# An RWKV-6 layer with a gated MLP on one core: level six and the state's products of steps six to eleven in one TensorE group

## The chip, the cores and the metric

The kernel runs on one core of one Trainium2 chip. The metric is the time on the device in microseconds, the median over runs. All arithmetic is fp32.

## The reference

Two blocks follow one another. The first is the RWKV-6 recurrence for 4 batches, 8 heads, 768 tokens and head size 48:

```
state = 0
for t in range(768):
    cur   = (u * k[t]) outer v[t]
    y[t]  = r[t] @ (state + cur)
    state = w[t][:, None] * state + k[t] outer v[t]
```

The decay w lies between 0.80 and 0.95 and differs by token and by channel. The second block takes the 3072 x 384 result x through a hidden layer of 2048:

```
h   = x @ w_in
g   = h * erf(softplus(h))
out = g @ w_out
```

## The kernel before, in words

The 768 tokens are cut into six chunks of 128, the four batches into two pairs, which makes twelve steps, numbered 0 to 11. A step takes one chunk of two batches: 256 token rows, 16 batch-head pairs. Steps with the same parity belong to the same pair of batches, so the state made in step s is used in step s + 2.

Inside a chunk the recurrence is a triangular matrix of products between receptances r and keys k, each faded by the decays between the two tokens. The kernel builds it in levels: level n pairs the left half of a block of 2^n tokens with its right half. A chunk is split into two halves of 64 tokens, so level six is the last. `level_products` makes a level's products on TensorE, `take_level` puts them into the tile `own` (a masked copy on VectorE up to level five, two plain copies on ScalarE for level six), and `scale` multiplies r and k of the next step's tile `in` by the products of decays that the level asks for. GpSimd makes those products of decays (`tot_sb`).

From step 5 on (`attend_late`), the levels one to four are not made by TensorE. Instead `prepare(s + 1)`, a generator, works in step s on the near products of the next step: for each distance 1 to 15 inside a block of 16 tokens it multiplies r by shifted keys (`term`, lines 463 and 467), sums over channels (`sum_up`, line 453), and fades the keys one token further. VectorE does the distances 1 to 4, GpSimd 5 to 15. The sums (`sums`) and the faded keys (`words`) then go through DRAM to be turned around: `k_blocks` and `by_blocks` are written, `by_tokens` and `kT` are read back, all on SyncE's queue (lines 499 to 509). `by_tokens` gives the first content of the next step's `own` (line 514). `kT` holds keys faded to the end of their block of 16; they still have to be faded to the end of their half of 64. For that `spread_blocks` turns `over_blocks`, a small tile of decay products, with a matmul against the identity, ScalarE copies the result (`few`), and two transfers spread it to every token (`g_rows`, `spread`). Line 718 multiplies `kT` by `spread`.

The products of faded keys with values give what a half adds to the state (`state_part`, line 659). The sums are `middle`, the state in the middle of the chunk (line 736), and `S_next`, that at its end (line 743), each from an old state faded by GpSimd (`faded`, lines 713 and 739) and the products in PSUM. `from_own` (line 584) and `through_state` (line 610) of a step run at the head of the following step: they make y in PSUM, the first from `own` and the values, the second from the states and r. `fence` (line 593) is a small VectorE copy between the two halves of `from_own`.

The MLP runs two and three steps behind, cut into pieces that are placed by hand between the groups of the attention. A letter string for each stage of a step says which pieces stand there:

- P: one of seven pieces of a projection (`project_fast`, line 1142), 16 matmul records of 192 columns
- H: one of eight pieces of the hidden layer (`hidden`, line 1027), 12 matmul records of 256 columns, with a ScalarE copy that empties the PSUM tile (line 1036); two such tiles (`m`) take turns
- s, ey, ep: softplus of a chunk, and erf of it into the PSUM lane y or the PSUM lane p, each with an activation table load on ScalarE
- m: VectorE's multiply of a chunk by its erf (line 992)
- k22y, k11p, k12y: ScalarE copies of quarters of a hidden tile into a lane (line 1100); S1 to S4: VectorE's sums of quarters (lines 1119 to 1125) for the projection
- F: one more part of `prepare`
- w: one sum of weights for the last two steps' hidden layer (line 1194)

The lane p is the PSUM tile pp1, the level products use pp0, and the lane y is the tile in which y is made. Each engine runs its instructions in the order in which they are written here; the stages of a step are "front", "near" and 0 to 4. The usual strings before the change are

```python
USUAL = (
    "s P", "m", "ey P m s P P ep P", "m k22y P F P k11p F F", "S1", "S2 S3 H k12y S4 H F",
    "s H ey m H H F s H ep H H",
)
```

Of the kernel before, what the change touches and what calls it, by code (L numbers as in the profile page):

```python
# [11 lines left out]
FP32 = mybir.dt.float32  # L12
# [49 lines left out]
def kernel(  # L62
# [47 lines left out]
    faded = [const.tile([P, JP, D], FP32, name="faded")] * NC  # L110
    seen = const.tile([P, NE * NP * NC], FP32, name="seen")

    over_blocks = const.tile([P, C // NEAR, JP], FP32, name="over_blocks")
    u_sb = const.tile([P, NP], FP32, name="u_sb")
    ident = const.tile([P, P], FP32, name="ident")
    mask_sb = const.tile([P, MASKED, HC], I32, name="mask_sb")
# [14 lines left out]
    def products(shape, n=None):  # L131


        if n is not None:
            return ps_p.tile(shape, FP32, name=f"pp{n}")
        n = turns["next"]
        turns["next"] = 1 - n
        return ps_p.tile(shape, FP32, name=f"pp{n}")
# [65 lines left out]
    def near_log(s):  # L204
        return NEAR_LOG - (s == DIRECT)
# [97 lines left out]
    def rows(e, n=D):  # L303
        return slice(e * EP, e * EP + n)
# [7 lines left out]
    def scale(s, level, batch=None):  # L312

        in_t, tots = loaded[s][0], ready[s][1]
        half, nb = 1 << (level - 1), JP * C >> level
        if batch is not None:
            nb //= NJ
            halves = view(
                turns["first"][:, batch], half, [[NP * C - half, 2], [2 * half, nb], [1, half]]
            )  # L320
            nc.vector.tensor_mul(
                halves, halves,
                view(tots[level - 1], 2 * batch * nb, [[1, 2], [2, nb], [0, half]]),
            )
            return
        n = 1 if s > DIRECT and level == LOG else 2
        halves = view(in_t[:, 0:2], half, [[JP * C - half, n], [2 * half, nb], [1, half]])
        nc.vector.tensor_mul(  # L328
            halves, halves, view(tots[level - 1], 0, [[1, n], [2, nb], [0, half]])
        )  # L330
# [23 lines left out]
    def prepare(s):  # L354
# [61 lines left out]
        if s == DIRECT:  # L416
            yield
        else:
            half = view(tots[NEAR_LOG + 1], 1, [[2, NC], [C >> NEAR_LOG + 1, JP]])
            quarter, last = (  # L420
                view(tots[NEAR_LOG], n, [[4, NC], [C >> NEAR_LOG, JP]]) for n in (1, 3)
            )
            to = over_blocks[:].rearrange("p (h b) n -> p b h n", h=NC)
            nc.gpsimd.tensor_mul(to[:, 0], quarter, half)
            nc.gpsimd.tensor_copy(out=to[:, 1], in_=half)
            nc.gpsimd.tensor_copy(out=to[:, 2], in_=last)
            yield
# [79 lines left out]
        if near == NEAR:  # L507
# [2 lines left out]
                out=kTs[s][:], in_=k_blocks[:].rearrange("(g b) s d -> (b s) g d", g=NH)  # L510
            )
        scale(s, near_log(s))
        nb = HC // NEAR
        nc.vector.tensor_mul(
            own[:].rearrange("p n (b t) -> p n b t", t=NEAR),
# [148 lines left out]
                        stop=True,  # L664
                    )

    def spread_blocks(s, pp):


        n = D // 2  # L670
        for e in range(NE):
            nc.tensor.matmul(
                pp[:EP, e, 0:2, HC // 2 : HC // 2 + n],
                lhsT=over_blocks[rows(e)].rearrange("p b n -> p (b n)"),
                rhs=ident[rows(e), rows(e)], start=True, stop=True,
            )
        few = att.tile([EP, NE * 2, n], FP32, name="few", bufs=1)
        nc.scalar.copy(
            few[:].rearrange("p (e i) d -> p e i d", e=NE),
            pp[:EP, :, 0:2, HC // 2 : HC // 2 + n],  # L680
        )
        g_rows = dram.tile([C // NEAR, JP * NE * D], FP32, name="g_rows")
        nc.sync.dma_start(
            out=g_rows[:].rearrange("b (n d) -> (b n) d", n=JP),
            in_=few[:].rearrange("p i d -> p (i d)"),
        )
        spread[s] = att.tile([P, JP, NE, D], FP32, name="spread", bufs=1)
        nc.sync.dma_start(
            out=spread[s][:].rearrange("p n e d -> p (n e d)"),
            in_=g_rows[:, None, :].to_broadcast([C // NEAR, NEAR, JP * NE * D]),  # L690
        )

    def attend_late(s, run):

        c, in_t, vt, own, S, S_next, ends = parts_of(s)
        RK = by_pair(in_t)
        before = s - 1 if s - 1 > DIRECT else None
        if before:
            from_own(before, ready[before][0], 1)
            fence()  # L700
        pp = products([P, NE, JP, HC], 0)
        level_products(pp, RK, LOG - 1)
        scale(s, LOG - 1)
        take_level(own, pp, LOG - 1)
        run("front", None)
        if before:
            from_own(before, ready[before][0], 0)
            through_state(before, xTs[before])
            if s + 1 < n_steps:
                load_step(s + 1)  # L710
        following = prepare(s + 1) if s + 1 < n_steps else iter(())
        next(following, None)
        nc.gpsimd.tensor_mul(faded[0][:], S[:], ends[:, :, 0:1].to_broadcast([P, JP, D]))
        next(following, None)
        run("near", None)
        next(following, None)
        kT = kTs[s]
        nc.vector.tensor_mul(
            kT[:].rearrange("p (e n) d -> p n e d", e=NE),
            kT[:].rearrange("p (e n) d -> p n e d", e=NE), spread[s][:],  # L720
        )
        run(0, following)

        pp = products([P, NE, JP, HC], 0)
        level_products(pp, RK, LOG)
        if s + 1 < n_steps:
            spread_blocks(s + 1, pp)
        take_level(own, pp, LOG)
        scale(s, LOG)
        run(1, following)  # L730
        ps = products([P, NC, JP, HC], 0)
        ps = [[ps[:, h]] * NE for h in range(NC)]
        state_part(s, kT, ps)
        run(2, following)
        for e in range(NE):
            nc.vector.tensor_add(middle[rows(e)], faded[0][rows(e)], ps[0][e][rows(e), :, :D])
        run(3, following)
        if s < n_steps - SPC:
            nc.gpsimd.tensor_mul(
                faded[1][:], middle[:], ends[:, :, 1:2].to_broadcast([P, JP, D])  # L740
            )
            for e in range(NE):
                nc.vector.tensor_add(S_next[rows(e)], faded[1][rows(e)], ps[1][e][rows(e), :, :D])
        run(4, following)

    def attend_first(xT):

# [572 lines left out]
    def in_order(s, k):  # L1320
# [3 lines left out]
        for what in order[k]:  # L1324
# [5 lines left out]
                piece(hids, s - 1)  # L1330


    STAGES_LATE = ("front", "near", 0, 1, 2, 3, 4)
    LATE = {
        DIRECT + 1: (
            "s ey", "m", "s ep m P P s ey m P P P", "s P F ep m P F P k22y k11p F", "S1",
            "S2 S3 H k12y S4 H F", "s H ep m H H F G s H H H ep",
        ),
        n_steps - 1: (
            "s P", "m w", "ey P m s P P ep P", "m P P", "", "", ""  # L1340
        ),
    }
    USUAL = (
        "s P", "m", "ey P m s P P ep P", "m k22y P F P k11p F F", "S1", "S2 S3 H k12y S4 H F",
        "s H ey m H H F s H ep H H",
    )

    def run_late(s, tokens, following=None):
# [64 lines left out]
    with tc.manual_schedule(  # L1413
# [74 lines left out]
        s = n_steps  # L1488
        from_own(s - 1, ready[s - 1][0], 1)
        fence()  # L1490
        run_late(s - 1, "S Q w w w")
        from_own(s - 1, ready[s - 1][0], 0)
        through_state(s - 1, xTs[s - 1])
        run_late(s, "P P P P T")
# [102 lines left out]
```

## Time and profile before

| what | value |
|---|---|
| time, median of 3 runs | 584.82 us (583.95 to 585.79) |
| profiled execution, its own time | 586.88 us |
| its span from the first to the last instruction | 585.1 us |
| TensorE busy | 576.4 us, 99% |
| VectorE busy | 454.7 us, 78% |
| ScalarE busy | 355.6 us, 61% |
| GpSimd busy | 274.1 us, 47% |
| starts of steps 6 to 11 (first `from_own` record) | 240.98, 285.73, 330.23, 374.73, 419.23, 463.71 us |

In the order of time of an engine a row gives the start in us from the beginning of the span, the duration of that run of instructions, the engine and the line, what is written and what is read, and in brackets how long the engine had been idle and what ended that. Merged rows can overlap the following row by a little, so lengths of pieces are taken from one start to the next. An fp32 matmul leaves two records. Busy time is an average over the whole execution: in the stretch of steps 6 to 11 VectorE is busy for some 40 of every 44.5 us.

### The profile page before, as it was taken

How to read it: one execution, taken by the hardware profiler on the slowest of the kernel's cores; microseconds unless marked ns; L12 is line 12 of the kernel's file. 1: busy time of each engine (PE TensorE's matmuls, PEld its weight loads, DVE VectorE, ACT ScalarE, POOL GpSimd, SP SyncE). 2: the span in 40 equal slices, each digit the busy share in tenths (PEclk: the TensorE clock that was granted, in tenths of full speed). 3: DMA queues.
4: the chain of work that ended last, by engine and by line, in shares of the span. 5: the costliest groups of instructions: out<-in, count | busy, mean ns of one | idle time of the engine just before them, and what ended most of it. 6: DMA issues, size and time to landing. Idle time of an engine off the chain costs nothing.

```text
span 585.1 us, 16663 instructions
## 1 busy us (share of the span) xinstructions
PE 576.4 (99%) x7240; PEld 495.1 (85%) x7240; DVE 454.7 (78%) x558; ACT 355.6 (61%) x478; POOL 274.1 (47%) x313
## 2 busy tenths in 40 slices
PE   8899999999999999999999999999999999999997
PEld 6588887688668758998898898898898899988997
DVE  6776886999996899799799799799799637256630
ACT  3658877644544598756766666665765771387700
POOL 4557391702398469659459459449549200000000
PEclk9999999999999999999999999999999999999999
DMA  8587571440433414334334334334331301000000
GB/s 269 177 273 281 201 235 44 183 154 10 145 95 116 117 55 156 63 116 165 74 111 169 74 108 172 75 108 136 74 108 55 74 8 36 2 0 2 28 27 29
DMA packets 54082, 63.25 MB, mean 108 GB/s; under 512 B 35160, under 2 KB 40568, under 8 KB 52984
## 3 DMA queue, kind: packets, MB, share of 16 engines
q1 hardware_dynamic: 53624, 61.98, 33.4%
q8 instruction: 57, 0.93, 0.6%
q10 hardware_dynamic: 384, 0.20, 0.1%
q14 instruction: 17, 0.14, 0.1%
HBM read 52.39 MB, written 8.69 MB: 104 GB/s over the span
## 4 chain that ended last, share of the span: by engine, by line
PE 95%; DVE 3%; issue 1%; ACT 0%; POOL 0%; DVEq 0%; POOLq 0%
PE m L1027 36%; PE m L1142 28%; PE m L1059 8%; PE pp L552 6%; PE pp L1230 4%; PE y L1230 2%; PE y L584 2%; PE pp L659 2%; PE y L610 2%; PE m L862 1%; PE pp L871 1%; PE pp L938 1%; DVE in L328 1%; DVE words L467 1%; PE pp L1142 0%
## 5 line engine op out<-in xcount | busy, mean ns | idle before, releaser
L1027 PE MATMUL m<-xT,w_in_sb 128*128 128x256 f32 x960 | 215.3, 382 | 0.1
L1027 PEld LDWEIGHTS m<-xT,w_in_sb 128*128 128x128 f32 x960 | 179.9, 190 | 26.2 <-issue 1.0
L328 DVE TENSOR_TENSOR in<-in,tot_sb 128x1024 f32<-128x1024 f32 (+1 forms) x55 | 75.3, 1369 | 16.5 <-PE pp L552 13.2
L463 POOL TENSOR_TENSOR rk<-words 128x528 f32<-128x528 f32 (+3 forms) x28 | 42.5, 1517 | 91.2 <-DVE sums L453 80.7
L1036 ACT COPY h<-m 128x512 f32<-128x512 f32 x80 | 46.4, 579 | 57.6 <-PE m L1027 57.5
L467 POOL TENSOR_TENSOR words<-words,rest 128x528 f32<-128x528 f32 (+10 forms) x77 | 78.1, 1015 | 6.0
L1059 PE MATMUL m<-w_out_sb,h 128*128 128x384 f32 x192 | 64.3, 491 | 0.0
L1059 PEld LDWEIGHTS m<-w_out_sb,h 128*128 128x128 f32 x192 | 35.7, 190 | 23.5
L1142 PE MATMUL m<-mixed,h 128*128 128x192 f32 x256 | 45.6, 331 | 0.0
L1142 PE MATMUL m<-w_out_sb,h 128*128 128x192 f32 x256 | 44.8, 329 | 0.0
L552 PEld LDWEIGHTS pp<-in 48*64 48x64 f32 (+1 forms) x2368 | 33.4, 126 | 12.0 <-issue 6.2
L1142 PEld LDWEIGHTS m<-mixed,h 128*128 128x128 f32 x256 | 41.4, 190 | 0.9
L1142 PEld LDWEIGHTS m<-w_out_sb,h 128*128 128x128 f32 x256 | 41.6, 190 | 0.3
L1142 PE MATMUL m<-w_out_sb,room 128*128 128x192 f32 x240 | 41.5, 326 | 0.0
L983 ACT ACT_TABLE_LOAD x30 | 38.5, 1283 | 2.7 <-issue 2.2
L987 ACT ACT_TABLE_LOAD x30 | 38.5, 1283 | 1.5 <-DVE room L1125 1.1
L1142 PEld LDWEIGHTS m<-w_out_sb,room 128*128 128x128 f32 x240 | 39.4, 190 | 0.0
L402 POOL TENSOR_TENSOR tot_sb<-tot_sb 128x256 f32<-128x256 f32 (+4 forms) x50 | 36.2, 724 | 3.8
L552 PE MATMUL pp<-in 48*64 48x32 f32 (+1 forms) x2368 | 37.3, 212 | 0.6 <-DVE in L328 0.5
L463 POOL TENSOR_TENSOR words<-words 128x336 f32<-128x336 f32 (+6 forms) x49 | 35.3, 720 | 3.8
L453 DVE TENSOR_REDUCE sums<-rk 128x14 f32<-128x672 f32 (+9 forms) x54 | 34.7, 701 | 0.0
L453 DVE TENSOR_REDUCE sums<-words 128x6 f32<-128x288 f32 (+8 forms) x66 | 26.9, 464 | 3.9 <-POOL words L463 3.6
(198 smaller groups left out, 951.5 us busy)
## 6 DMA issues: line engine op xcount, KB each, us to landing
in<-in_rkw SPq DMA_DIRECT2D x8, 1024.0 KB, 5.1
words<-in_moe_w_in SPq DMA_DIRECT2D x16, 384.0 KB, 5.4
words<-in_moe_w_out SPq DMA_DIRECT2D x16, 384.0 KB, 4.7
words<-in_rk_rows SPq DMA_DIRECT2D x8, 768.0 KB, 5.6
w<-in_rkw SPq DMA_DIRECT2D x11, 512.0 KB
v<-in_v SPq DMA_DIRECT2D x12, 384.0 KB, 5.6
out<-o SPq DMA_DIRECT2D x23, 192.0 KB, 2.4
in<-in_rkw SPq DMA_DIRECT2D x7, 512.0 KB, 5.7
```

What stands on the lines that cost most here:

```text
L328: nc.vector.tensor_mul(halves, halves, view(tots[level - 1], 0, [[1, n], [2, nb], [0, half]]))
L402: nc.gpsimd.tensor_mul(new, pair[:, :, 0], pair[:, :, 1])
L453: nc.vector.tensor_reduce(out=view(sums[:], n, [[near * (NEAR + 1), NEAR // near], [NEAR + 1, near - n]]), in_=terms[n], axis=mybir.AxisLi ...
L463: engine.tensor_mul(terms[n], r[:, :, n:], k[:, :, : near - n])
L467: engine.tensor_mul(k[:, :, :m], k[:, :, :m], w[:, :, n : n + m])
L552: nc.tensor.matmul(to, lhsT=rk(1, n)[rows(e), s0 : s0 + m], rhs=right, start=True, stop=True,)
L983: nc.scalar.activation(sp_room, chunks[0], AF.Softplus)
L987: nc.scalar.activation(at, sp_room, AF.Erf)
L1027: nc.tensor.matmul(ps[:, ff, :], lhsT=w_in_sb[:, g * FG + f + ff, kk * P : (kk + 1) * P], rhs=xT[:, kk, :], start=kk == 0, stop=kk == KT - 1,)
L1036: nc.scalar.copy(h[:, f : f + FT, :], ps[:])
L1059: nc.tensor.matmul(ps[j][:], lhsT=gs[g][:, f, j * C : (j + 1) * C], rhs=w_out_sb[:, g * FG + f, :], start=g + f == 0, stop=g == NG - 1 and ...
L1142: nc.tensor.matmul(to, lhsT=a[:, f], rhs=b[:, f], start=start and f == 0, stop=f == FG - 1, skip_group_check=True,)
```

## The change

From step 6 on, five things are different.

1. The level-six products and the state's products follow one another directly, in a new stage "mid" behind `through_state`, with the piece "ey P" in front of them. The state's products are written to pp1, since pp0 holds level six. ScalarE's two copies of level six stand between the first erf (ey) and the softplus of stage 0.
2. `spread_blocks` stays at its place, now alone among projection pieces, as one matmul of 128 rows and 96 columns against the identity in place of two of 48 rows. For this `over_blocks` has 128 columns.
3. The state's sums (`sum_states`) stand together before the near sums of the next step. The fading of `middle` for `S_next` goes from GpSimd to VectorE, in step 5 too.
4. The multiply of `kT` by `spread` (`fade_keys`) is written at the end of the step before, behind the multiply of the last erf (lane p) and the first content of `own`, for which `prepare` has one more `yield`.
5. In step 11 the one w of the stage "near" goes to the tail, where four stand together.

Step 5 keeps its order, but for the sums and for its last stage, where the second ep stands one H piece earlier and m and F follow.

```diff
@@ prepare @@
         scale(s, near_log(s))
+        yield
         nb = HC // NEAR
@@ spread_blocks @@
+        if pp is None:
+            got = products([P, NE * JP * HC], 0)[:, : NE * D].rearrange("p (e d) -> p e d", e=NE)
             nc.tensor.matmul(
-                pp[:EP, e, 0:2, HC // 2 : HC // 2 + n],
-                lhsT=over_blocks[rows(e)].rearrange("p b n -> p (b n)"),
-                rhs=ident[rows(e), rows(e)], start=True, stop=True,
+                got, lhsT=over_blocks[:].rearrange("p i b n -> p (i b n)"),
+                rhs=ident[:].rearrange("p (e m) -> p e m", e=NE)[:, :, :D],
+                start=True, stop=True,
             )
+            nc.scalar.copy(few[:], got[:EP])
...
@@ attend_late @@
+        run("mid", None)
+
+        def state():
+            ps = products([P, NC, JP, HC], 1 if before else 0)
+            state_part(s, kTs[s], [[ps[:, h]] * NE for h in range(NC)])
+            return ps
+
+        def sum_states(ps):
+            for h, into in enumerate((middle, S_next)):
+                if h and s >= n_steps - SPC:
+                    continue
+                if h:
+                    nc.vector.tensor_mul(
+                        faded[1][:], middle[:], ends[:, :, 1:2].to_broadcast([P, JP, D])
+                    )
+                for e in range(NE):
+                    nc.vector.tensor_add(
+                        into[rows(e)], faded[h][rows(e)], ps[rows(e), h, :, :D]
+                    )
+
+        if before:
+            pp = products([P, NE, JP, HC], 0)
+            level_products(pp, RK, LOG)
+            ps = state()
+            take_level(own, pp, LOG)
         following = prepare(s + 1) if s + 1 < n_steps else iter(())
         next(following, None)
         nc.gpsimd.tensor_mul(faded[0][:], S[:], ends[:, :, 0:1].to_broadcast([P, JP, D]))
         next(following, None)
         run("near", None)
+        if before:
+            sum_states(ps)
         next(following, None)
-        kT = kTs[s]
-        nc.vector.tensor_mul(
-            kT[:].rearrange("p (e n) d -> p n e d", e=NE),
-            kT[:].rearrange("p (e n) d -> p n e d", e=NE), spread[s][:],
-        )
+        if not before:
+            fade_keys(s)
         run(0, following)
...
+        elif s + 1 < n_steps:
+            spread_blocks(s + 1)
         scale(s, LOG)
...
         run(4, following)
+        for _ in following:
+            pass
+        if s + 1 < n_steps:
+            fade_keys(s + 1)
+
+    def fade_keys(s):
+
+        kT = kTs[s][:].rearrange("p (e n) d -> p n e d", e=NE)
+        nc.vector.tensor_mul(kT, kT, spread[s][:])
@@ the strings @@
-    STAGES_LATE = ("front", "near", 0, 1, 2, 3, 4)
+    STAGES_LATE = ("front", "mid", "near", 0, 1, 2, 3, 4)
     USUAL = (
-        "s P", "m", "ey P m s P P ep P", "m k22y P F P k11p F F", "S1", "S2 S3 H k12y S4 H F",
-        "s H ey m H H F s H ep H H",
+        "s P", "ey P", "", "m s P P ep P", "m k22y P F P k11p F F", "S1", "S2 S3 H k12y S4 H F",
+        "s H ey m H H F s H ep H H m F",
     )
-        run_late(s - 1, "S Q w w w")
+        run_late(s - 1, "S Q w w w w")
```

## The prediction

> **What bounds the kernel now.** I read the page first, then the order of time of each engine over one whole step (step 8, which begins at 330.23 us), then the transfers. The page's chain of waits:
>
> ```profile
> PE 95%; DVE 3%; issue 1%; ACT 0%; POOL 0%; DVEq 0%; POOLq 0%
> ```
>
> TensorE sets the end. Its order of time over step 8 (start, duration, instruction):
>
> ```profile
> 331.73 2.87 PE L1142 MATMUL m<-w_out_sb,h 128*128 128x192 f32 x16
> ...
> 346.61 0.76 PE L552 MATMUL pp<-in 48*32 48x32 f32 x64
> 347.30 0.32 PE L672 MATMUL pp<-ident,over_blocks 48*64 48x48 f32 x4
> 347.55 2.87 PE L1142 MATMUL m<-mixed,h 128*128 128x192 f32 x16
> ...
> 352.94 0.94 PE L659 MATMUL pp<-v,kT 64*48 64x48 f32 x64
> 353.81 20.99 PE L1027 MATMUL m<-xT,w_in_sb 128*128 128x256 f32 x96
> 374.73 0.66 PE L584 MATMUL y<-own,v 64*48 64x64 f32 x32
> ```
>
> There is no hole: a step lasts 374.73 - 330.23 = 44.50 us. So cheaper TensorE work pays in full, but only while VectorE keeps up. VectorE and GpSimd over the same step:
>
> ```profile
> 333.62 0.94 DVE L470 TENSOR_TENSOR words<-words,u_row 128x768 f32<-128x768 f32 x1
> ...
> 341.29 1.21 DVE L992 TENSOR_TENSOR h<-h,pp 128x1024 f32<-128x1024 f32 x1
> 342.42 2.37 DVE L453 TENSOR_REDUCE sums<-rk 128x15 f32<-128x720 f32 x3
> ...
> 347.22 1.72 DVE L718 TENSOR_TENSOR kT<-kT,spread 128x768 f32<-128x768 f32 x1
> ...
> 357.71 1.21 DVE L1119 TENSOR_TENSOR room<-h,y 128x1024 f32<-128x1024 f32 x1
> 358.84 1.11 DVE L736 TENSOR_TENSOR middle<-faded,pp 48x384 f32<-48x384 f32 x2
> ```
> ```profile
> 343.40 1.31 POOL L463 TENSOR_TENSOR rk<-words 128x528 f32<-128x528 f32 x1 [14.52 <-DVE sums L453]
> ...
> 366.69 0.28 POOL L467 TENSOR_TENSOR words<-words,rest 128x48 f32<-128x48 f32 x1
> ```
>
> GpSimd's near products of step 9 start 0.98 us after VectorE's first sums (342.42) and keep it going to 366.97. Then SyncE's queue takes the finished keys through DRAM:
>
> ```profile
> 367.00 0.33 SPq L499 DMA_DIRECT2D k_blocks<-words  x1
> 367.45 0.36 SPq L501 DMA_DIRECT2D by_blocks<-sums  x1
> 369.74 0.37 SPq L503 DMA_DIRECT2D by_tokens<-by_blocks  x1
> 370.21 0.99 SPq L509 DMA_DIRECT2D kT<-k_blocks  x1
> ```
> ```profile
> kT<-k_blocks SPq DMA_DIRECT2D x1, 384.0 KB, 4.7
> ```
>
> The keys land at 370.21 + 4.7 = 374.9, just after step 9 began, yet line 718 first needs them a whole stage later, some 17 us of slack. In step 6 (from 240.98) ScalarE shows a second place where little is left:
>
> ```profile
> 270.28 1.02 ACT L1100 COPY y<-h 128x1024 f32<-128x1024 f32 x1 [2.24 <-DVE room L1119]
> 271.23 0.58 ACT L1036 COPY h<-m 128x512 f32<-128x512 f32 x1
> ```
>
> The copy that empties a hidden layer's PSUM tile stands behind a lane copy, and that waits for S1 (line 1119) on VectorE. The second hidden piece's tile was ready at about 269.9 and is read until 271.81; the fourth piece, 2.6 us behind the third, needs it at 272.5.
>
> **What the Trainium skill says.** "TensorEngine Tiling (Array Packing)", Key Properties: a change of tiling mode drains TensorE. The trace agrees in direction: a projection piece between two of its own kind takes 2.60 us from start to start (338.72, 341.32), one between two small groups 2.79 (331.73 to 334.52). "SBUF — State Buffer", Who interferes with whom: a VectorE instruction with two SBUF inputs and a GpSimd instruction that reads SBUF exclude each other for a whole instruction. The trace agrees: line 718 takes 1.72 us beside GpSimd and 0.96 in step 11, where GpSimd rests. "DMA: Bandwidth & Descriptors", Anatomy of one DMA: about 2 us of a transfer are fixed. The 16 KB xT transfers take 1.9 us to land, so a shorter wait for kT can't be hoped for.
>
> **The change part by part.** Sums go against the profiled execution (span 585.1, its time 586.88, 2.06 above the median 584.82); the difference goes onto the median.
>
> *TensorE.* Matmuls keep their number but for the spread, four records of 48 rows (0.25 us, 347.30 to 347.55) that become two of 128 rows and 96 columns. The trace has no such form. The nearest row is the projection's, 16 records of 192 columns in 2.60 us, 0.1625 each: two cost 0.16 us if time goes with the columns and 0.33 if the weight load sets it; I take 0.20, nearer the columns, because small groups show that loads can run faster than 0.16 each. Level six and the products are adjacent: 0.69 + 0.87 kept. Of the seven projection pieces (18.78 us in step 8) two now stand between small groups (2 x 2.79), one behind one (2.71), four between their own kind (4 x 2.60): 18.69. The hidden pieces lose the switch at their front: 20.92 to 20.82. Step: 44.50 - 0.05 - 0.09 - 0.10 = 44.26. Bounds: 0 to 0.4 saved.
>
> *ScalarE.* The same copies, softplus and erf. Level six's two copies (1.16 us) now wait for TensorE, done 9.3 us into the step; softplus with its table load (2.3) then ends at 13.0, and the piece's copy behind it (0.46) by 13.5. The piece that needs that copy starts at 15.4: hidden by two pieces, dear only if ScalarE is 1.9 us late.
>
> *VectorE.* The fading of S_next moves here from GpSimd (0.83 there): line 467 takes 0.76 for 576 columns and 0.90 for 720, so 384 come to some 0.57 (between 0.50, in proportion, and GpSimd's 0.83). The state's sums are 1.14 + 0.59 + 1.13 = 2.86 and now stand ahead of the near sums, where a 1.13 multiply stood: those, and GpSimd behind them, start 1.7 later. The multiply of the second erf, own (now no longer waiting for by_tokens in the middle of the step) and line 718 go to the end of the step before. Line 718 waits there for kT, and behind it in VectorE's queue stand the fence, scale of level five, level five's masked copy and everything of the next step. That closes a loop which had been open.
>
> *The loop*, from the end f of line 718 to the next: fence 0.20 + scale 1.14 + copy 0.61 = 1.95; nine near products 341.29 - 333.62 = 7.67; state sums 2.86; to GpSimd's start 0.98; GpSimd 23.60 (343.40 to 367.00) less some 0.58, because line 718 no longer takes the port from it (the 480-column product beside it took 1.80 against 1.22): 23.02; k_blocks to kT's issue 3.21; landing 4.7 + 0.19 (own starts at 372.93, by_tokens landed 3.0 after 369.74); line 718 beside an idle GpSimd 0.90. Sum 45.48 us, 1.22 above TensorE's 44.26.
>
> *Where TensorE meets it.* S1 starts at f + 12.48 (to the near sums) + 4.80 (rest of sums, 342.42 to 347.22) + 1.13 + 0.60 + 1.13 + 0.46 + 1.64 + 0.46 + 3.42 (the rows from 348.86 to 357.71) = f + 26.12. Then 1.24 to the lane copy, 0.95 + 0.58 for it and the hidden copy behind it, 0.1: the fourth hidden piece starts at f + 29.0. Softplus (2.25 with its table load) and a copy (0.6) stand before the fifth, so 31.85 where TensorE was ready at 31.6; erf and a copy before the sixth, 34.7 for 34.45. With five pieces of 2.61 and those 0.5 the step ends at f + 42.6. The fence needs f + 0.3 at 4.3 us into the step, level six f + 2.0 at 8.6: with f 2.9 us into the step both are in time.
>
> *Course.* In step 5 the sums inserted delay the near sums to 235.9, so by_blocks goes then, by_tokens 2.2 later, kT 0.47, and f(6) = 238.5 + 4.7 + 0.19 + 0.90 = 244.3. Step 7 begins at 244.3 + 42.6 = 286.9 (285.73 before), step 8 at 332.4 (330.23), step 9 at 377.9, step 10 at 423.3 (419.23). In step 10 half the state falls away, 1.72 us less, so step 11 begins one free TensorE step later, 467.6 (463.71 before): +3.9. Step 11 has no near products and no loop; it and the tail cost 0.05 less. The join of weights moved to the tail adds 1.2 us on VectorE ahead of the tokens' joins; those end at 498.96 and TensorE wants the first at 504.86: hidden by 5.9. Median 584.82 + 3.85 = 588.7 us.
>
> **The rivals.**
> *A, the loop decides* (my case): a loop L from 44.7 to 46.2 gives, by the same course, a step 11 1.5 to 6.0 later and 586.3 to 590.8. For it: every row of the loop is in the trace. Against: 1.22 is the small difference of two large sums.
> *B, the loop closes inside TensorE's step* (not slower). Place: line 718's wait for kT. It needs a loop of at most 44.3, that is 1.2 us less: near products or GpSimd faster where they no longer share the port. Then 0.24 for six steps, and 0.25 of a ScalarE wait in step 6: some 583.2; half closed, 585.
> *C, the loop is longer.* GpSimd keeps 23.6, and its totals of the next step run beside line 718 (1.64): L = 46.8. Step 11 then begins at 244.3 + 4 x 46.8 + 40.9 = 472.4: +8.7, 593.5.
> *D, the copy of level six holds up ScalarE*: softplus waits for TensorE's group, pieces wait for their copy. Above a lateness of 1.9 us each counts; 0.7 us in six steps less the gain gives 588. Nothing in the rows asks for it.
> That the group doesn't come together isn't a case: both products are issued in one run.
>
> **How the numbers follow.** A 0.68, B 0.17, C 0.11, D 0.04. What a measurement can tell from no change is 0.3%, 1.75 us: 583.1 to 586.6. B lies around the lower edge: 0.06 faster, 0.11 same; A's low end gives 0.04 to same. Faster 0.06, same 0.15, slower 0.79. A's own range is 586.3 to 590.8; with most of B and up to C, 583.6 to 593.5.
>
> **What would show it.** Right: VectorE idle ahead of line 718 "DMA kT", about 1 us a step; TensorE's step 45.3 to 45.6 in steps 7 to 9 with holes in the hidden pieces (line 1027's idle put down to ScalarE's h), and 44.3 in step 11; GpSimd's first product some 14.7 us into a step instead of 13.2; the hidden row of 96 at 20.8 where nothing waits. Wrong: TensorE whole at 44.3 with kT landed ahead of line 718 (B), holes at the fence or level five (C), holes in the projection pieces (D).

## The result, and the profile after

The changed kernel takes 588.81 us (587.45 to 589.34, median of 6 runs) against 585.41 us (583.95 to 586.12, 6 runs) for the kernel before: a ratio of 1.0058, interval 1.0041 to 1.0075. It is slower, by some 3.4 us. A repetition beside the experiments gave 587.82 against 585.05, ratio 1.0041 (1.0029 to 1.0053). The profiled execution took 588.25 us, with a span of 586.4.

Up to the first projection record of step 5 the change hardly touches the kernel, and yet the profiled executions of this case differ there by 3 us (it stands at 194.1 to 197.2 us). So the parts of two profiles are compared from that record on. "Repeated" is a second profiled execution of the changed kernel.

| us | before | changed | changed, repeated |
|---|---|---|---|
| rest of step 5 | 43.82 | 45.56 | 44.75 |
| steps 6 to 10 | 222.73 | 225.02 | 224.93 |
| step 11 | 23.16 | 23.32 | 23.32 |
| the tail | 98.23 | 98.20 | 98.20 |
| sum | 387.94 | 392.10 | 391.20 |

The repeated execution is 3.26 us longer: 0.93 in step 5, 2.20 in steps 6 to 10, 0.16 in step 11, less 0.03 in the tail. The first one has a further 0.8 in step 5. Of the other kernels with the same step 5 one has it too (45.53), the rest take 44.70 to 44.97; in the two long ones S1 stands 28.23 and 28.26 us behind the first projection record, in the repeated execution 27.27. The lengths of steps 6 to 10 are

| us | 6 | 7 | 8 | 9 | 10 |
|---|---|---|---|---|---|
| before | 44.75 | 44.50 | 44.50 | 44.50 | 44.48 |
| changed | 45.45 | 45.02 | 45.05 | 45.07 | 44.43 |
| changed, repeated | 45.48 | 45.04 | 45.07 | 45.08 | 44.26 |

In the rows of a profile PE is TensorE and PEld its weight loads, DVE is VectorE, ACT ScalarE, POOL GpSimd, and SP SyncE; a q behind the name stands for the engine's queue. L1061 is line 1061 of that kernel's text; the lines of the kernels differ by some numbers. The page's chain of waits of the changed kernel, shares of the span by engine:

```profile
PE 53%; DVE 7%; ACT 3%; issue 2%; DMA 1%; ACTq 0%; SPq 0%; DVEq 0%
```

TensorE had 95% of this chain, and now VectorE, ScalarE and a transfer stand in it. (Followed back from the end it reaches only to about 195 us here, so its shares add up to some 66%.) TensorE's order of time over step 8 (start, duration, instruction):

```profile
330.35 0.66 PE L585 MATMUL y<-own,v 64*48 64x64 f32 x32
...
338.93 0.76 PE L553 MATMUL pp<-in 48*32 48x32 f32 x64
339.62 0.94 PE L660 MATMUL pp<-v,kT 64*48 64x48 f32 x64
340.49 2.87 PE L1176 MATMUL m<-w_out_sb,room 128*128 128x192 f32 x16
...
348.39 0.36 PE L674 MATMUL pp<-ident,over_blocks 128*128 128x96 f32 x2
348.58 2.79 PE L1176 MATMUL m<-mixed,h 128*128 128x192 f32 x16
351.21 2.76 PE L1176 MATMUL m<-w_out_sb,h 128*128 128x192 f32 x16
353.81 21.66 PE L1061 MATMUL m<-xT,w_in_sb 128*128 128x256 f32 x96
375.40 0.67 PE L585 MATMUL y<-own,v 64*48 64x64 f32 x32
```

The group is there: level six and the state's products take 0.69 and 0.87, start to start, and the spread 0.19 as two records. Up to the hidden layer nothing is late: it begins 23.46 us into the step (23.58 before). But its 96 records last 21.59 us from start to start where before they lasted 20.92. The waits of steps 7 to 9 say for whom (engine, line, cause: us in total, times, longest):

```profile
PEld m L1061 <- ACT h L1070: 3.5, 9, 0.4
...
DVE kT L778 <- DMA kT<-k_blocks: 1.2, 3, 0.5
```

Three times a step a hidden piece, the fourth, the fifth and the sixth, waits for the copy that empties its PSUM tile. And once a step VectorE waits for kT. VectorE's order of time over the same step (in brackets: idle before, and what ended it):

```profile
330.93 0.96 DVE L778 TENSOR_TENSOR kT<-kT,spread 128x768 f32<-128x768 f32 x1 [0.34 <-DMA kT<-k_blocks]
331.80 0.17 DVE L594 COPY seen<-y 128x16 f32<-128x16 f32 x1
331.99 1.23 DVE L328 TENSOR_TENSOR in<-in,tot_sb 128x1024 f32<-128x1024 f32 x1
...
341.42 1.11 DVE L734 TENSOR_TENSOR middle<-faded,pp 48x384 f32<-48x384 f32 x2
...
344.31 2.38 DVE L453 TENSOR_REDUCE sums<-rk 128x15 f32<-128x720 f32 x3
...
350.37 1.50 DVE L328 TENSOR_TENSOR in<-in,tot_sb 128x512 f32<-128x512 f32 x1
...
358.90 1.21 DVE L1153 TENSOR_TENSOR room<-h,y 128x1024 f32<-128x1024 f32 x1
...
373.28 1.22 DVE L1026 TENSOR_TENSOR h<-h,pp 128x1024 f32<-128x1024 f32 x1 [2.96 <-ACT pp L1021]
374.42 1.22 DVE L515 TENSOR_TENSOR own<-block_sb,by_tokens 128x1024 f32<-128x1024 f32 x1
376.12 0.96 DVE L778 TENSOR_TENSOR kT<-kT,spread 128x768 f32<-128x768 f32 x1 [0.48 <-DMA kT<-k_blocks]
```

Line 778 is the multiply that was line 718, line 1153 is S1, and lines 730 and 734 are the state's sums. Two closed ways lead from this step into the next.

*The kT loop.* From line 778 (330.93) to scale (331.99), the near products, the state's sums, the near sums (344.31), GpSimd's start (345.29), its end and k_blocks (368.22), kT's issue (371.43) and 4.69 us later line 778 again: 376.12 - 330.93 = 45.19, and 44.94 in the step before. The mean, 45.07, is the step. The rows of GpSimd's start and of SyncE's queue:

```profile
345.29 1.31 POOL L463 TENSOR_TENSOR rk<-words 128x528 f32<-128x528 f32 x1 [16.80 <-DVE sums L453]
```
```profile
368.22 0.33 SPq L499 DMA_DIRECT2D k_blocks<-words  x1
...
371.43 1.05 SPq L509 DMA_DIRECT2D kT<-k_blocks  x1
```

*The S1 loop.* From the step's start (330.35) 1.64 to scale, which needs TensorE's level five; 26.91 to S1; 1.24 to ScalarE's lane copy (360.14); 0.96 to the copy of the second hidden piece behind it (361.10), which takes 0.58; and from its end the fourth hidden piece and what follows, some 13.7 to the next start at 375.40. Sum 45.05. ScalarE works without a gap from the lane copy to the copy ahead of the sixth hidden piece (366.80), so a later S1 also comes through to the sixth piece, the last that waits. The first two rows of ScalarE:

```profile
360.14 1.02 ACT L1134 COPY y<-h 128x1024 f32<-128x1024 f32 x1 [2.96 <-DVE room L1153]
361.10 0.58 ACT L1070 COPY h<-m 128x512 f32<-128x512 f32 x1
```

In the kernel before the second way was 1.64 + 25.84 + 1.24 + 0.95 + 0.58 + 13.7 = 43.95: half a microsecond of slack under TensorE's 44.50. The stretch from scale to S1 grew by 1.07: 2.89 for the state's sums, less 1.64 (line 718 gone) and 1.13 (a multiply gone), and 0.8 for a row whose work nobody changed, level six's scale (128 x 512), which took 0.60 from start to start before and takes 1.41 now; 0.14 are small differences of other rows, most of it in the near sums.

Both loops share the stretch from scale to the near sums on VectorE, and both have the length of the step. Which of them holds it can't be read from this profile: that is what most experiments are for.

Step 5 has a hole of its own. ScalarE and TensorE there:

```profile
229.02 1.28 ACT L1021 ACT_TABLE_LOAD   x1 [0.83 <-DVE h L1157]
```
```profile
231.91 8.04 PE L1061 MATMUL m<-xT,w_in_sb 128*128 128x256 f32 x36 [0.81 <-ACT h L1070]
```

The first erf of the lane p waits for S3 (line 1157), which reads that lane, and a hidden piece's copy stands behind the erf. S3 now starts 5.15 us behind S1 (227.73 - 222.58) and started 3.41 behind it before (227.90 - 224.49), since all the state's sums stand between S1 and S2, where only those of `middle` stood.

### The profile page after: what moved, and what is told of

The parts are those of the page before. It is cut to its first block, busy times and chain, and to the rows that moved or that the text cites. A ratio compares the mean times of both kernels' runs of the same rounds, so it can differ in the third digit from the quotient of the medians.

```text
span 586.4 us, 16630 instructions
## 1 busy us (share of the span) xinstructions
PE 578.0 (99%) x7230; PEld 493.6 (84%) x7230; DVE 457.5 (78%) x563; ACT 356.9 (61%) x478; POOL 264.8 (45%) x308
## 4 chain that ended last, share of the span: by engine, by line
PE 53%; DVE 7%; ACT 3%; issue 2%; DMA 1%; ACTq 0%; SPq 0%; DVEq 0%
PE m L1176 25%; PE m L1061 17%; PE pp L1264 4%; PE y L1264 2%; DVE in L328 2%; PE pp L553 1%; DVE sums L453 1%; PE y L585 1%; PE y L611 1%; DMA kT<-k_blocks 1%; PE pp L660 1%; ACT room L1017 1%; ACT L1021 1%; ACT L1017 1%; DVE words L467 0%
## 5 line engine op out<-in xcount | busy, mean ns | idle before, releaser
L1061 PE MATMUL m<-xT,w_in_sb 128*128 128x256 f32 x960 | 218.3, 383 | 1.3 <-ACT h L1070 1.2
L1061 PEld LDWEIGHTS m<-xT,w_in_sb 128*128 128x128 f32 x960 | 178.9, 190 | 31.8 <-ACT h L1070 7.3
L328 DVE TENSOR_TENSOR in<-in,tot_sb 128x1024 f32<-128x1024 f32 (+1 forms) x55 | 78.7, 1430 | 4.8 <-PE pp L553 3.0
L467 POOL TENSOR_TENSOR words<-words,rest 128x528 f32<-128x528 f32 (+10 forms) x77 | 75.5, 980 | 6.0
L1026 DVE TENSOR_TENSOR h<-h,pp 128x1024 f32<-128x1024 f32 x15 | 18.2, 1214 | 22.3 <-ACT pp L1021 22.3
L1134 ACT COPY y<-h 128x1024 f32<-128x1024 f32 x12 | 12.2, 1017 | 37.4 <-DVE h L1026 20.7
```

Of the source, the lines that this page charges most:

```text
L328: nc.vector.tensor_mul(halves, halves, view(tots[level - 1], 0, [[1, n], [2, nb], [0, half]]))
L467: engine.tensor_mul(k[:, :, :m], k[:, :, :m], w[:, :, n : n + m])
L1061: nc.tensor.matmul(ps[:, ff, :], lhsT=w_in_sb[:, g * FG + f + ff, kk * P : (kk + 1) * P], rhs=xT[:, kk, :], start=kk == 0, stop=kk == KT - 1,)
```

## The experiments

The theory that the prediction had was the kT loop alone. The expectations below say which theories they set against each other. Each row of the table stands beside the kernel before on the same chip.

| kernel | us | before | ratio (interval) | steps 7 to 9 |
|---|---|---|---|---|
| changed, fade at its old place | 590.96 | 584.84 | 1.0092 (1.0066 to 1.0118) | 45.87 to 45.89 |
| changed, sums behind the near sums | 588.87 | 584.84 | 1.0065 (1.0044 to 1.0087) | 45.14 to 45.16 |
| before, with the fade moved alone | 584.38 | 584.84 | 0.9994 (0.9981 to 1.0008) | 44.50 |
| changed, GpSimd's work shortened | 588.43 | 584.84 | 1.0056 (1.0037 to 1.0075) | 45.02 to 45.05 |
| changed, S1 earlier | 586.74 | 584.59 | 1.0031 (1.0017 to 1.0044) | 44.96 to 45.17 |
| changed, 1.26 more ahead of the sums | 595.82 | 584.59 | 1.0185 (1.0151 to 1.0218) | 46.26 to 46.28 |
| changed, 1.26 more behind S1 | 588.41 | 584.59 | 1.0066 (1.0045 to 1.0087) | 45.00 to 45.03 |
| changed, level six's copies later | 587.89 | 584.59 | 1.0058 (1.0035 to 1.0081) | 45.02 to 45.03 |
| changed, again | 587.82 | 585.05 | 1.0041 (1.0029 to 1.0053) | 45.04 to 45.08 |
| changed, S1 earlier and GpSimd shortened | 585.48 | 585.05 | 1.000 (0.9982 to 1.0017) | 44.28 to 44.33 |
| changed, S1 earlier and fade at its old place | 587.04 | 585.05 | 1.0026 (1.0013 to 1.0040) | 44.78 to 44.81 |
| changed, sums back at their old places | 591.84 | 584.40 | 1.0124 (1.0107 to 1.0141) | 45.90 to 45.91 |

### The fade at its old place

```diff
         take_level(own, pp, LOG - 1)
+        if before:
+            fade_keys(s)
         run("front", None)
...
-        if s + 1 < n_steps:
-            fade_keys(s + 1)
```

> The changed kernel, with the multiply of kT by spread moved from the end of step s to step s + 1, behind level five's masked copy. Theory 1 (the loop over line 718's wait for kT sets the step): fence, scale and masked copy, 1.85 us, run while kT is on its way, the loop falls from 45.05 to some 43.2, TensorE sets the step again: 44.3 in steps 7 to 9, about 1.2 us below the kernel before. Theory 2 (a second loop, over ScalarE, is nearly as long: S1, lane copy, copy of the second hidden piece, softplus, erf, the last multiply by the erf, own): only the wait for kT, 0.34 to 0.48 us a step, goes; steps 7 to 9 take 44.6 to 44.7 and the time stands within 0.5 us of the middle between both kernels' less a little, some 587.3 where the changed kernel takes 588.8. Theory 3 (holes come from level six's copies on ScalarE): no change, 588.8.

Measured: 590.96 us, steps of 45.88, and no wait for kT any more. Every expectation missed. The kT loop is open and the step is longer than in the changed kernel. TensorE's hidden pieces, and S1 on VectorE, in step 8:

```profile
354.65 8.04 PE L1061 MATMUL m<-xT,w_in_sb 128*128 128x256 f32 x36 [0.38 <-DVE o L1196]
362.87 13.73 PE L1061 MATMUL m<-xT,w_in_sb 128*128 128x256 f32 x60 [0.18 <-ACT h L1070]
```
```profile
360.05 1.21 DVE L1153 TENSOR_TENSOR room<-h,y 128x1024 f32<-128x1024 f32 x1
```

VectorE waits 0.74 for TensorE ahead of scale (at 332.30), so a step's start sets S1's time: S1 comes 27.75 behind scale, 0.84 later than in the changed kernel, because the fade (0.86) now lies in between. The step grew by the same 0.8. So another way holds the step as soon as kT doesn't: the S1 loop, and the wait for line 1196, which reads the PSUM tile of the first hidden piece, on the same stretch of VectorE. (Line 1196 is VectorE's sum of the sixth projection piece.) The edit itself makes the S1 loop longer; the shortened GpSimd below opens the kT loop without that. The prediction's theory, that the kT loop alone costs the time, falls.

### The state's sums behind the near sums

```diff
         run("near", None)
+        next(following, None)
         if before:
             sum_states(ps)
-        next(following, None)
```

> The changed kernel, with the state's five VectorE sums behind the near sums in place of ahead of them. GpSimd starts 2.9 us earlier. Theory 1: the loop falls to 42.2 us, TensorE sets the step with 44.3, about 1.2 us below the kernel before. Theory 2: S1 comes no earlier, so the loop over ScalarE keeps 44.6 to 44.7 us, some 587.3. Theory 3: 588.8.

Here GpSimd starts some 2.9 us earlier, and kT isn't waited for. The step stays at 45.15, since S1 stands where it stood, 27.02 us behind scale (26.91 in the changed kernel). The holes are those of the first experiment, for line 1196 (up to 0.5 us) and for ScalarE's h. The last that waits is again the sixth hidden piece; it begins 37.19 us into the step, and 37.08 in the changed kernel.

### The kernel before, with the fade moved alone

```diff
-        nc.vector.tensor_mul(
-            kT[:].rearrange("p (e n) d -> p n e d", e=NE),
-            kT[:].rearrange("p (e n) d -> p n e d", e=NE), spread[s][:],
-        )
+        if not before:
+            fade_keys(s)
...
+        for _ in following:
+            pass
+        if s + 1 < n_steps:
+            fade_keys(s + 1)
```

> The kernel before, with one part of the change alone: the multiply of kT by spread stands at the end of the step before, behind own. The loop is closed here too, but without the state's sums in it (2.88) and with a multiply by an erf (1.13): 43.3 us. Theory 1 and 2: TensorE's 44.5 us a step stays, time that of the kernel before within 0.3%. A theory in which the waiting multiply at the head of VectorE's queue is itself what costs would say 1 us or more slower.

584.38 us, steps of 44.50: no difference. VectorE's rows at the end of step 8:

```profile
371.11 0.96 DVE L751 TENSOR_TENSOR kT<-kT,spread 128x768 f32<-128x768 f32 x1 [0.64 <-DMA kT<-k_blocks]
...
373.05 1.22 DVE L328 TENSOR_TENSOR in<-in,tot_sb 128x1024 f32<-128x1024 f32 x1 [0.74 <-PE pp L552]
```

Line 751, the moved fade, waits for kT, and scale behind it still waits 0.74 for TensorE. A wait for kT in the queue is no cost by itself; it costs from the point at which scale no longer waits for TensorE. In the changed kernel that reserve is used up, at 331.99 and 0.34 to 0.48 of wait.

### GpSimd's work shortened

From the near products of step 7 on, distances 12 to 15 are left out: their products and their sums.

```diff
-            term(nc.gpsimd, *range(9, NEAR))
+            few_left = NEAR if s <= DIRECT + 2 else 12
+            term(nc.gpsimd, *range(9, few_left))
...
-            sum_up(*range(5, NEAR))
+            sum_up(*range(5, few_left))
```

> The changed kernel, in which from step 6 on the near products of the distances 12 to 15 of the following step are left out, with their sums (the keys are then not faded to the end and the result differs). GpSimd ends about 3.7 us earlier, and kT with it; nothing ahead of S1 changes on VectorE. Theory 1: no wait for kT, TensorE's 44.3 us a step, 1.2 us below the kernel before. Theory 2: the loop over ScalarE remains, 44.6 to 44.7 us a step, some 587.3. Theory 3: 588.8.

The keys leave 33.68 us into step 8, where they left at 37.87, kT isn't waited for, and scale waits 0.5 for TensorE again. The step is 45.02 to 45.05 all the same, and the hidden pieces wait for h just as before (3.4 us, nine times in three steps, against 3.5). VectorE's order is untouched up to S1. So the S1 loop alone holds 45.03, through TensorE.

### S1 earlier

```diff
-        "s P", "ey P", "", "m s P P ep P", "m k22y P F P k11p F F", "S1", "S2 S3 H k12y S4 H F",
+        "s P", "ey P", "", "m s P P ep P", "m k22y P F P k11p S1 F F", "", "S2 S3 H k12y S4 H F",
```

> The changed kernel, with S1 (line 1153) placed ahead of the last two scales of stage 1, 3.4 us earlier on VectorE; nothing else moves. Theory 4, formed after the first runs: the step is set by a loop that goes through TensorE itself: start of the step, level five, scale, everything on VectorE up to S1, lane copy, copy of the second hidden piece, fourth hidden piece, next start: 1.64 + 26.91 + 1.24 + 1.53 + 13.7 = 45.05 us in the changed kernel. With S1 3.4 us earlier it falls to 41.6, and TensorE's own 44.3 us stay: the time is that of the kernel before less 1 to 1.5 us. Theory 1 (the wait for kT closes the loop): GpSimd's chain is as long as before, 45.05 us a step stay, 588.8. If the wait for kT comes next it grows by 0.8 us a step from the 1.6 us at which it stands, which the 4.0 us up to the fence take in for three steps.

S1 now stands ahead of two scales (3.35 us). Step 6 falls to 44.48, but steps 7 to 9 stay at 44.96 to 45.17. VectorE ahead of step 8 and TensorE in it:

```profile
330.41 0.96 DVE L778 TENSOR_TENSOR kT<-kT,spread 128x768 f32<-128x768 f32 x1 [0.77 <-DMA kT<-k_blocks]
```
```profile
352.85 20.99 PE L1061 MATMUL m<-xT,w_in_sb 128*128 128x256 f32 x96 [0.62 <-DVE o L1196]
```

The hidden pieces run through (20.92 from start to start), the wait for kT grows to 0.7 to 0.8, and the hole moves to the front of the hidden layer, where line 1196, late with all of VectorE, still reads the tile. So the kT loop alone holds 45.04 as well. Each loop is long enough for the whole loss: opening one shows the other.

### Both opened

The edits of the last two kernels together, so distances 12 to 15 are left out here too.

> S1 early, and GpSimd's distances 12 to 15 with their sums left out (so the result differs): both loops open in one kernel, where each of the two edits alone left 45.0 us a step. Theory 5 (two loops of the same length, one through kT, one through S1; either alone holds the step): neither is left, steps 7 to 9 fall to 44.3, TensorE's own, and step 6 to at most 44.5. A theory in which some third thing gives the 45.0 (TensorE's group itself, ScalarE): 45.0 as before.

Busy time of the engines in steps 7 to 9 of this kernel, and in step 8 of the changed one:

```profile
core 0: us, PE busy (x) PEld busy (x) DVE busy (x) ACT busy (x) POOL busy (x), PEclk, DMA share, GB/s
286.35:330.65 44.30, 44.30 (x531) 40.88 (x530) 39.67 (x48) 29.45 (x37) 22.80 (x24) 1.00 0.39 117
330.65:374.93 44.28, 44.28 (x532) 40.86 (x531) 39.68 (x48) 29.52 (x37) 22.81 (x24) 1.00 0.39 117
374.93:419.26 44.33, 44.33 (x531) 40.88 (x531) 39.66 (x48) 29.53 (x37) 22.80 (x24) 1.00 0.35 105
```
```profile
330.35:375.40 45.05, 45.05 (x532) 40.60 (x531) 40.85 (x52) 29.56 (x37) 26.22 (x32) 1.00 0.38 115
```

44.28 to 44.33: TensorE's own step, with no wait in its list, 0.2 below the kernel before. With either edit alone the step is 45.03 or 45.04, so the two loops are in parallel, and their lengths agree to some hundredths. The "busy" column of TensorE hides this: it says 45.05 of 45.05 for the changed kernel, because short waits lie inside merged records. The lengths of the pieces and the list of waits show it. The whole time is only that of the kernel before, 585.48 against 585.05: in the profile steps 6 to 10 are 1.08 shorter, but step 5 is 0.93 longer, as in the changed kernel, and step 11 with the tail 0.13.

Opened without leaving work out, with the fade at its old place, S1 earlier, and one projection piece ahead of the second erf's multiply:

```diff
-        "s P", "ey P", "", "m s P P ep P", "m k22y P F P k11p F F", "S1", "S2 S3 H k12y S4 H F",
+        "s P", "ey P", "", "m s P P ep P", "P m k22y F P k11p S1 F F", "", "S2 S3 H k12y S4 H F",
```

> The changed kernel with nothing left out: the multiply of kT by spread behind level five's masked copy of the next step (opens the loop through kT), S1 ahead of the last two scales (opens the loop through S1), and the sixth projection piece ahead of the multiply by the second erf, so that its sum (line 1196) frees its PSUM tile 1.1 us earlier for the first hidden piece. Theory 5: 44.3 us a step from 6 to 10, 1.2 to 1.5 us below the kernel before, some 583.3 where that takes 584.6. If VectorE's chain up to line 1196, 22.9 us into the step by the sum of the rows against 23.5 when TensorE needs the tile, is longer than worked out, the holes stand at the first hidden piece and the step takes 44.5.

44.78 to 44.81 a step, a miss by 0.3 to 0.5. TensorE's hidden layer, its weight loads at the sixth hidden piece, and ScalarE's first erf in step 8:

```profile
354.04 21.39 PE L1061 MATMUL m<-xT,w_in_sb 128*128 128x256 f32 x96
367.39 7.64 PEld L1061 LDWEIGHTS m<-xT,w_in_sb 128*128 128x128 f32 x36 [0.48 <-ACT h L1070]
```
```profile
364.51 1.28 ACT L1021 ACT_TABLE_LOAD   x1 [1.50 <-DVE room L1159]
```

The sixth hidden piece begins 36.82 us into the step, and 36.41 where the loops are opened by leaving work out and nothing waits. It waits for ScalarE's copy behind the first erf, and the erf for S4 (line 1159). S4 comes 31.00 behind scale instead of 30.14, since the fade is back on this stretch. By these waits there is a third way, through the same stretch of VectorE and on to S4; no run opens it. The second hidden piece waits too, for line 1201, but that delays it by 0.06 only.

### An added cost on VectorE, ahead of the sums and behind S1

A reduction that nothing uses, 1.35 us (1.26 from start to start), at two places:

```diff
         if before:
+            nc.vector.tensor_reduce(
+                out=seen[:, 0:3], in_=w_out_sb[:, 0:3, :], axis=mybir.AxisListType.X, op=ALU.add,
+            )
             sum_states(ps)
```

> The changed kernel, with one more VectorE instruction of about 1.2 us in each of the steps 6 to 11, ahead of the state's sums and so ahead of S1: a sum over 1152 columns of the weights, which nobody uses. Theory 4: the loop grows by all of it, steps 6 to 9 by 1.2 us each, step 10 by some 0.2, about 593.7 where the changed kernel takes 588.8. Theory 1: GpSimd starts 1.2 us later, the loop over kT grows just as much, the same 593.7, with the wait for kT ahead of line 778 still there. Theory 3: 588.8.

```diff
         scale(s, near_log(s))
+        if s > DIRECT + 2:
+            nc.vector.tensor_reduce(
+                out=seen[:, 0:3], in_=w_out_sb[:, 0:3, :], axis=mybir.AxisListType.X, op=ALU.add,
+            )
         yield
```

> The changed kernel with the same unused VectorE sum, placed behind S1 to S4, where VectorE then waits 3 us for ScalarE's last erf (steps 6 to 10). All theories of a loop: the wait takes it in, 588.8 within 0.5 us; if instead VectorE's load as such were what costs, 5 us more, as in the run with the filler ahead of S1.

Ahead of the sums the 1.26 cost 1.22 a step: 46.26 to 46.28. Behind S1, in the same queue, they cost nothing, 45.00 to 45.03. There VectorE waits for the last erf, and this wait gives way, from 2.97 to 1.72:

```profile
373.73 1.22 DVE L1030 TENSOR_TENSOR h<-h,pp 128x1024 f32<-128x1024 f32 x1 [1.72 <-ACT pp L1025]
```

So it is the place on VectorE that counts, the stretch from scale to S1. A miss in the first of the two: step 10 took 45.38 where little more than the changed kernel's 44.26 to 44.43 was expected. The expectation had scale 1.64 us into the step. It comes at 2.51, because kT is waited for at the step's head (1.16); that is so in the changed kernel too (2.51 and 2.83), but there S1 is early enough to hide it, and with the filler ahead of it S1 isn't.

### Level six's copies later

ScalarE's two copies go behind the softplus of stage 0 (the letter t).

```diff
-            take_level(own, pp, LOG)
+            turns["take"] = lambda: take_level(own, pp, LOG)
...
-        "s P", "ey P", "", "m s P P ep P", "m k22y P F P k11p F F", "S1", "S2 S3 H k12y S4 H F",
+        "s P", "ey P", "", "m s t P P ep P", "m k22y P F P k11p F F", "S1", "S2 S3 H k12y S4 H F",
```

> The changed kernel, with ScalarE's two copies of level six behind the softplus of stage 0 in place of ahead of it. Theory 3 (that copy's wait for TensorE's group holds up softplus and the projection): up to 0.7 us a step less, 585 to 586. Theory 4 and 1: ScalarE had 1.9 us to spare there, 588.8 within 0.5 us.

587.89 us, steps of 45.02 and 45.03: the place of these copies is worth nothing.

### The sums back, the group kept

Level six in pp1 and the state's products in pp0, so that the sums can stand where they stood before, split between two stages; the spread goes to a free part of pp0, behind the second hidden piece (the letter x).

```diff
-            ps = products([P, NC, JP, HC], 1 if before else 0)
+            ps = products([P, NC, JP, HC], 0)
...
-            pp = products([P, NE, JP, HC], 0)
+            pp = products([P, NE, JP, HC], 1)
...
-        if before:
-            sum_states(ps)
...
-            spread_blocks(s + 1)
+            turns["x"] = lambda: spread_blocks(s + 1, room=ps[:, 0])
...
-        if not before:
-            sum_states(ps)
+        sum_states(ps, 0, middle)
         run(3, following)
+        sum_states(ps, 1, S_next)
...
-        "s P", "ey P", "", "m s P P ep P", "m k22y P F P k11p F F", "S1", "S2 S3 H k12y S4 H F",
+        "s P", "ey P", "", "m s P P ep P", "m k22y P F P k11p F F", "S1", "S2 S3 H k12y S4 H x F",
```

> The changed kernel with its group kept and the state's sums put back: level six goes to pp1 and the state's products to pp0, the sum for the middle stands behind S1 and that for the end behind the near sums of GpSimd's part (as in the kernel before, in step 5 too), and the spread's matmul goes behind the second hidden piece, into the part of pp0 that the middle's sum has read. By theory 5 2.9 us leave both loops, 42.2 us each, and TensorE's own 44.3 us are left in steps 6 to 10. Step 5, which the changed kernel lengthens from 43.8 to 44.75 us (from the first projection record to the start of step 6), returns to 43.8, if it is the sums between S1 and S3 there that ScalarE's erf waits for. Together 1.2 us below the kernel before, a ratio of 0.998. If the group itself, or line 718's early place, costs something of its own, steps 6 to 10 stay at 44.5 or more.

591.84 us, steps of 45.9: a miss with a wait of its own. TensorE at the spread, and VectorE's sum for `middle`:

```profile
361.27 0.43 PE L674 MATMUL pp<-ident,over_blocks 128*128 128x96 f32 x2 [1.36 <-POOL words L463]
```
```profile
360.01 1.11 DVE L732 TENSOR_TENSOR middle<-faded,pp 48x384 f32<-48x384 f32 x2
```

TensorE stands 1.36 us ahead of the spread until VectorE has read `middle`'s products from that PSUM tile (361.12). The row puts the wait down to GpSimd, which nothing there asks for; in step 6 the same row names line 732. So this kernel says nothing on the loops. It does settle step 5: with the sums split as before, that step took 43.81 from its first projection record, as in the kernel before, and the hidden layer ran through in 20.98 from start to start (20.99 before).

No kernel here beats the one before; that with the fade moved alone equals it, and so does the one with both loops opened, which leaves work out. None keeps the group with all the work and runs at TensorE's own step; whether one can stays open.

## Why the prediction was right or wrong

**The time** was right: 588.81 for 588.7, and slower. Its rise of 3.85 us was 3.40, but it was put together differently: steps 6 to 10 cost 2.20 where 3.9 were forecast, step 5 0.93 where nothing was, and step 11 and the tail 0.13 where 0.05 were to be gained. That the sum comes within 0.1 us of the measured time is luck.

**TensorE** was right. The spread takes 0.19 (0.20 said), and where nothing waits, in step 10 of the repeated profile and with both loops opened, a step takes 44.26 to 44.33 (44.26 said) and the hidden layer 20.81 (20.82 said).

**ScalarE** was right: rival D is refuted by the copies put later. GpSimd's first product stands 14.94 us into the step (14.7 said).

**The loop** was right in its rows and off in its size: 45.07 instead of 45.48. Of the difference, the transfer with its wait took 4.69 instead of 4.89, GpSimd 22.93 instead of 23.02, and the fence little over 0.1 instead of 0.20. So the wait at kT was 0.34 to 0.48 where about 1 was said; ahead of it VectorE waits 2.96 for ScalarE's last erf, which the prediction didn't look at.

**"Where TensorE meets it"** is the step that failed. The kT loop is there, and with S1 early it holds the step at 45.04 by itself; what the prediction missed is that it isn't the only one. It worked out the S1 path and used it only to carry the kT loop's delay to TensorE, as if S1 hung on kT. But scale also waits for TensorE's level five, 1.64 into the step, so the path closes on itself without kT. It had 0.5 us of slack in the kernel before, and got 1.07 more; with the shortened GpSimd, where kT isn't waited for, it gives 45.02 to 45.05 by itself. The runs show two loops of the same length; the prediction had one, and the time was near because both say nearly the same.

Closing the path would not have been enough: with the prediction's own figures it is 42.6 - 0.20 + 1.64 = 44.04 us, below TensorE's 44.26. The row that turned it was sized by its old neighbourhood. S1 was put at 25.92 us behind scale (26.12 less the fence's 0.20); it came at 26.91. Of these 0.99, 0.81 are level six's scale, taken at 0.60 from the old order and 1.41 in the new, and 0.12 the near sums.

**Rival B** (the loop closes inside the step) was worked out with one loop only. The shortened GpSimd gave the shorter kT loop that it asked for, and the step stayed at 45.03.

**Step 5** was wrong: "the sums inserted delay the near sums" was followed, but not S3 behind them, ScalarE's erf behind S3, and the copy behind the erf.

**Step 10** was right: half the state falls away and the step returns to 44.26 to 44.43; the text calls it "step 11" once, for the one that ends where step 11 begins.

## What to carry to other kernels

In a kernel whose steps overlap, list every closed way from one step's start to the next, with its length, also those that have some slack now: a change that adds work to an engine with idle time is paid where that engine's stretch lies on such a way (1.22 of 1.26 us here), and free elsewhere in the same queue. Two loops of equal length look like one: an experiment that opens one and shows no gain doesn't acquit it; only opening both shows what they cost. Before sums are moved, follow each instruction behind them to the engine that waits for it, in the steps before and after the loop too.

## What the runs showed of the hardware that was not expected

A VectorE instruction's time went with what GpSimd did at that moment, in both directions. Level six's scale on VectorE (128 x 512, two inputs in SBUF) took 0.68 before and 1.50 now, with no change to itself. Before, it began at 350.00, just as a row of GpSimd ended (348.20 + 1.80), and went ahead of the next. Now it begins at 350.37, inside a row (350.11 + 1.21 = 351.32), and ends at 351.87, 0.55 behind that row. The rows before, and GpSimd's row now:

```profile
350.00 0.68 DVE L328 TENSOR_TENSOR in<-in,tot_sb 128x512 f32<-128x512 f32 x1
```
```profile
348.20 1.80 POOL L467 TENSOR_TENSOR words<-words,rest 128x480 f32<-128x480 f32 x1
```
```profile
350.11 1.21 POOL L467 TENSOR_TENSOR words<-words,rest 128x480 f32<-128x480 f32 x1
```

That fits the exclusion that the prediction cites from the Trainium skill ("SBUF — State Buffer", Who interferes with whom) for the fade. The other kernels agree: wherever this row began 0.10 to 0.29 us behind the start of a GpSimd row it ended 0.55 behind that row's end and took 1.44 to 1.61, in the kernel before with the fade moved alone too; in the one step where it began within 0.01 of a GpSimd row's start (step 10 with the sums behind the near sums) it took 0.68. Unexpected is that so small a shift between two engines' orders more than doubles a row, and that this was three quarters of what the path gained. The fade (128 x 768) went the other way, 1.72 to 0.96, now that GpSimd rests beside it, and GpSimd's own 480-column product from 1.80 to 1.21.

Joining two small groups cost and saved little: level six and the state's products keep 0.69 and 0.87 side by side, as they had apart, and a projection piece takes 2.60 between its own kind, 2.70 behind one small group and 2.79 between two.
